# A build-time list scheduler for block-sparse attention followed by a multiplicative FFN

## The chip, the cores and the metric

The kernel runs on one core of one Trainium2 chip. The metric is the device time of one execution in microseconds (us). "Span" is the time from the first to the last instruction in the profiled execution; the timed run is about 2 us longer than its span. One of the first runs of the kernel before took 429.86 us and is left out as an outlier. All ratios below are between runs whose state was fast.

## The reference

Attention with a block mask over 4 batches, 8 heads, 768 positions and head size 64, then an FFN without a nonlinearity other than a product. Cut to what matters:

```python
scores = (q @ k.T) / sqrt(64)             # per batch and head, 768 x 768
mask: |block_i - block_j| <= 1, first or last block row or column, three random blocks a row (32 x 32 blocks)
attn = softmax(where(mask, scores, -1e9))
x = (attn @ v) as [3072, 512]             # heads side by side
out = ((x @ w1) * (x @ w2)) @ w3 @ w_out  # w1, w2: 512 x 1024; w3: 1024 x 1024; w_out: 1024 x 512
```

## The kernel before

All matmuls are bf16. The kernel computes scores transposed (keys on partitions), takes exp on ScalarE (ACT), multiplies by a 0/1 mask on VectorE (DVE), and multiplies by v. `w3 @ w_out` is folded into one matrix on the way (the "weight fold"). The work of TensorE (PE) comes in three kinds, which use the 128 x 128 array in three shapes: scores (64 rows), values (32 columns, four matmuls side by side), and full-array matmuls, that is, the weight fold and the FFN. (The start has two small kinds more, the transposes of q and k and the mask tiles.)

An *attention unit* here is one (batch, 256 queries, half of the heads): three *groups*, each with two score units (4 matmuls each) and one *value third* (24 matmuls), all three thirds accumulating in the same two PSUM tiles `o` and `d`, of which there is one buffer each. A *filler piece* is four FFN matmuls of 512 columns. There are 24 units and 144 FFN pieces. PSUM also has two buffers for scores and two for filler.

```python
def scores(b, t, Q, kp, i):
    s = ps_s.tile([128, 2, 512], F32, ...)            # ps_s: 2 buffers
    for k2 in range(2):
        for h in range(2):
            nc.tensor.matmul(s[:, h, ...], lhsT=qk[64*h:64*h+64, 1, ...], rhs=qk[64*h:64*h+64, 0, ...], ...)
    e = epool.tile([128, 2, 512], BF16, ...)
    nc.scalar.activation(e, s, AF.Exp, scale=1.0 / 8.0)
    nc.vector.tensor_tensor(e, e, mask[:, t, kp:kp + 1, :]..., op=ALU.mult)

def normalize(b, t, Q):                               # frees the accumulators o and d
    nc.scalar.activation(ln, d, AF.Ln)
    nc.scalar.activation(rec[:, 0, :], ln, AF.Exp, scale=-1.0)
    nc.vector.tensor_tensor(X[i][...], o..., rec..., op=ALU.mult)
# [...]
for s, g in enumerate(groups):                        # 72 groups
    scores(b, t, Q, kp, 0)
    scores(b, t, Q, kp, 1)
    if prev is not None:
        values(*prev)                                 # one value third, of the group before
        finish(prev)                                  # after the last third: normalize, queue FFN pieces
    # [... loads of the next batch, transposes of pairs 2 and 3 ...]
    pop(0 if s < 3 else 2)                            # two filler pieces
    prev = g
while fill: pop(1)                                    # the FFN that is left: the tail
```

Before that loop stands the start: q and k come by DMA with a cast to bf16 on GpSimd's (POOL's) queue, DVE builds the 24 x 24 block table in some 25 small instructions, PE expands it to nine mask tiles, which ACT copies, and only then do scores begin. Each engine runs its instructions in the order of the program.

The softmax here doesn't subtract the row's maximum and nothing guards it: scores larger than these inputs give would overflow.

Of the kernel before, what the change touches and what calls it, by code (L numbers as in the profile page):

```python
# [13 lines left out]
PSUM = bass.MemoryType.PSUM  # L14


@with_exitstack
def kernel(
# [15 lines left out]

    nc = tc.nc
# [8 lines left out]
    NT = S // QT  # L44

    def pool(name, bufs, **kw):
# [7 lines left out]
    epool = pool("epool", 6)  # L54
# [3 lines left out]
    apool = pool("apool", 3)  # L58
# [3 lines left out]
    ps_f = pool("ps_f", 2, space=PSUM)  # L62

    order = tc.manual_schedule(
        engines={mybir.EngineType.PE, mybir.EngineType.Activation, mybir.EngineType.DVE}
    )
    order.__enter__()

    nc.scalar.preload_act_table_set("natural_log_exp_and_others")
# [5 lines left out]
    NP = H // 2  # L75
    qn, kn, vn = {}, {}, {}

    rand_sb = const.tile([NB, 6], I32, tag="rand_sb")
    nc.sync.dma_start(out=rand_sb, in_=sampled_blocks.bitcast(I32))

    def load_pair(b, pr, which="qkv"):
        for src, dst, pl, tag in ((qv, qn, nat, "qn"), (kv, kn, nat, "kn"), (vv, vn, natv, "vn")):
            if tag[0] in which:
                t = pl.tile([128, 2, C, D], BF16, tag=tag, name=tag)
                nc.gpsimd.dma_start(out=t, in_=src[b][:, 2 * pr:2 * pr + 2])  # L85
                dst[b, pr] = t
# [8 lines left out]
    def load_w12(ap, t):  # L95
        src = ap.rearrange("(Q g s d) f -> g d Q s f", Q=2, g=4, s=2)
        for g in range(4):
            for Q in range(2):
                nc.gpsimd.dma_start(out=t[32 * g:32 * g + 32, 2 * Q:2 * Q + 2, :], in_=src[g][:, Q])  # L99


    load_pair(0, 0, "qk")
    idf = const.tile([128, 128], F32, tag="idf")
    nc.gpsimd.iota(idf, pattern=[[-1, 128]], base=0, channel_multiplier=1,
                   allow_small_or_imprecise_dtypes=True)
    load_pair(0, 1, "qk")
    hotf = const.tile([NB, C, 128], F32, tag="hotf")
    nc.gpsimd.iota(hotf, pattern=[[1, C], [C, 128]], base=0, channel_multiplier=-BLK,
                   allow_small_or_imprecise_dtypes=True)
    JJ = const.tile([NB, NB], F32, tag="JJ")  # L110
    nc.gpsimd.iota(JJ, pattern=[[1, NB]], base=0, channel_multiplier=0,
                   allow_small_or_imprecise_dtypes=True)
    II = const.tile([NB, NB], F32, tag="II")
    nc.gpsimd.iota(II, pattern=[[0, NB]], base=0, channel_multiplier=1,
                   allow_small_or_imprecise_dtypes=True)
    load_pair(0, 0, "v")
    load_pair(0, 1, "v")
    wo_v = moe_w_out.rearrange("(c r) f -> r c f", r=128)
    nc.gpsimd.dma_start(out=wo_sb, in_=wo_v)

    def load_w3(lo, hi):
        for i in range(lo, hi):
            nc.gpsimd.dma_start(out=w3_sb[:, i, :], in_=moe_w3[128 * i:128 * i + 128, :])

    load_w3(0, 2)
    load_pair(0, 2)
    load_w3(2, 4)
    load_pair(0, 3)
    load_w3(4, NF)
    load_w12(moe_w1, w1_sb)  # L130
    load_w12(moe_w2, w2_sb)

    ident = const.tile([128, 128], BF16, tag="ident")
    nc.vector.tensor_scalar(ident, in0=idf, scalar1=0.0, scalar2=None, op0=ALU.is_equal)
    ones = const.tile([128, 32], BF16, tag="ones")
    nc.vector.memset(ones, 1.0)
    hot = const.tile([NB, C, 128], BF16, tag="hot")
    hot_hi = const.tile([NB, C, 128], BF16, tag="hot_hi")
    nc.vector.tensor_scalar(hot, in0=hotf, scalar1=0.0, scalar2=None, op0=ALU.is_ge)
    nc.vector.tensor_scalar(hot_hi, in0=hotf, scalar1=float(BLK), scalar2=None, op0=ALU.is_lt)  # L140
    nc.vector.tensor_tensor(hot, hot, hot_hi, op=ALU.mult)
    DD = const.tile([NB, NB], F32, tag="DD")
    nc.vector.tensor_sub(DD, II, JJ)

    A = const.tile([NB, NB], F32, tag="A")
    nc.vector.tensor_tensor(DD, DD, DD, op=ALU.mult)
    nc.vector.tensor_scalar(A, in0=DD, scalar1=1.0, scalar2=None, op0=ALU.is_le)
    for src in (II, JJ):
        for val, op in ((0.0, ALU.is_le), (float(NB - 1), ALU.is_ge)):
            t1 = small.tile([NB, NB], F32, tag="m24", name="m24")  # L150
            nc.vector.tensor_scalar(t1, in0=src, scalar1=val, scalar2=None, op0=op)
            nc.vector.tensor_max(A, A, t1)
    rand_f = const.tile([NB, 3], F32, tag="rand_f")
    for r in range(3):
        nc.vector.tensor_copy(rand_f[:, r:r + 1], rand_sb[:, 2 * r:2 * r + 1])
        t1 = small.tile([NB, NB], F32, tag="m24", name="m24")
        nc.vector.tensor_tensor(t1, JJ, rand_f[:, r:r + 1].to_broadcast((NB, NB)),
                                op=ALU.is_equal)
        nc.vector.tensor_max(A, A, t1)
    Ab = const.tile([NB, NB], BF16, tag="Ab")  # L160
    nc.vector.tensor_copy(Ab, A)
# [3 lines left out]
    gp = ps_s.tile([128, 2, 512], F32, tag="s", name="gp")  # L165
    for i, (lo, n) in enumerate(((0, 512), (512, 256))):
        nc.tensor.matmul(gp[:NB, i, :n], lhsT=Ab, rhs=hot2[:, lo:lo + n], start=True, stop=True)
        nc.vector.tensor_copy(G[:, lo:lo + n], gp[:NB, i, :n])
    mask = const.tile([128, NT, 3, 512], BF16, tag="mask")

    def build_mask(t):
        for kp in range(3):
            mp = ps_f.tile([128, 512], F32, tag="f", name="mp")
            for k2 in range(2):
                nc.tensor.matmul(mp[:, k2 * QT:(k2 + 1) * QT], lhsT=hot[:, 2 * kp + k2, :],  # L175
                                 rhs=G[:, t * QT:(t + 1) * QT], start=True, stop=True)
            nc.scalar.copy(mask[:, t, kp, :], mp)  # L177


    QK = {}  # L180

    def transposes(b, pr):
        tp = ps_s.tile([128, 2, 1024], BF16, tag="s", name="tp")
        for x, src in ((0, qn[b, pr]), (1, kn[b, pr])):
            for c in range(C):
                for h in range(2):
                    nc.tensor.transpose(tp[64 * h:64 * h + 64, x, c * 128:(c + 1) * 128],
                                        src[:, h, c, :], ident)
        t = qkt.tile([128, 2, S], BF16, tag="qkt", name="qkt")
        nc.vector.tensor_copy(t, tp[:, :, :S])  # L190
        QK[b, pr] = t

    qd, kd = (x.rearrange("b h (p c) d -> b p c h d", c=C) for x in (q, k))

    def load_pair_t(b, pr):
        load_pair(b, pr, "v")
        t = qkt.tile([128, 2, S], BF16, tag="qkt", name="qkt")
        for x, src in enumerate((qd, kd)):
            n = nat.tile([128, C, 2, D], BF16, tag="nt", name="nt")
            for h in range(2):  # L200
                nc.gpsimd.dma_start(out=n[:, :, h, :], in_=src[b][:, :, 2 * pr + h, :])  # L201
            nc.sync.dma_start_transpose(out=t[:, x, :].rearrange("r (c p) -> r c p", c=C),
                                        in_=n.rearrange("p c h d -> p (c h d)"))
        QK[b, pr] = t

    E = {}

    def scores(b, t, Q, kp, i):
        qk = QK[b, 2 * Q + i]
        s = ps_s.tile([128, 2, 512], F32, tag="s", name="s")  # L210
        for k2 in range(2):
            kc = 2 * kp + k2
            for h in range(2):
                nc.tensor.matmul(s[:, h, k2 * QT:(k2 + 1) * QT],  # L214
                                 lhsT=qk[64 * h:64 * h + 64, 1, kc * 128:(kc + 1) * 128],
                                 rhs=qk[64 * h:64 * h + 64, 0, t * QT:(t + 1) * QT],
                                 start=True, stop=True)
        e = epool.tile([128, 2, 512], BF16, tag="e", name="e")
        nc.scalar.activation(e, s, AF.Exp, scale=1.0 / 8.0)  # L219
        nc.vector.tensor_tensor(e, e, mask[:, t, kp:kp + 1, :].to_broadcast((128, 2, 512)),  # L220
                                op=ALU.mult)
        E[b, t, Q, kp, i] = e
# [3 lines left out]
    def values(b, t, Q, kp):  # L226
        if kp == 0:
            acc["o"] = ps_o.tile([128, 512], F32, tag="o", name="o")
            acc["d"] = ps_o.tile([128, QT], F32, tag="d", name="d")
        o, d = acc["o"], acc["d"]  # L230
        es = [E.pop((b, t, Q, kp, i)) for i in range(2)]
        for k2 in range(2):
            kc = 2 * kp + k2
            first, last = kc == 0, kc == C - 1
# [14 lines left out]
    X = {}  # L249
# [93 lines left out]
    for t in range(NT):  # L343
        build_mask(t)
# [47 lines left out]
    while fill:  # L392
        pop(1)
# [31 lines left out]
```

## Time and profile before

288.69 us, median of three runs (288.67, 288.69, and the outlier). The profiled run took 288.58 us.

| | PE | ACT | DVE |
|---|---|---|---|
| busy, us of the span of 286.8 | 260.8 | 188.8 | 183.8 |
| share | 91% | 66% | 64% |

The first part of the page: busy time by engine; then the span in 40 slices, the busy share of each in tenths, and the clock granted to PE.

```profile
PE 260.8 (91%) x3124; PEld 132.3 (46%) x3124; DVE 183.8 (64%) x296; ACT 188.8 (66%) x250; POOL 71.5 (25%) x105
...
PE   0478888898999999999999999999999999999994
...
PEclk9986999999999999999999999999999999999998
```

PE is the busiest, and nearly full from about 75 us (slice 11) on. Before that it is not. The same by stage; the columns are the stretch, its length, the busy time of PE, PE's weight loads, DVE, ACT and POOL with the number of instructions, the granted clock, the DMA share and GB/s.

```profile
0.00:20.00 20.00, 7.40 (x70) 4.50 (x72) 7.95 (x30) 5.52 (x10) 11.71 (x23) 0.98 0.97 140
20.00:75.00 55.00, 47.71 (x730) 27.05 (x729) 38.57 (x65) 39.08 (x48) 34.34 (x50) 0.95 1.42 166
75.00:240.00 165.00, 163.07 (x2066) 81.98 (x2066) 117.19 (x173) 130.50 (x172) 25.42 (x32) 1.00 0.60 73
240.00:300.00 60.00, 42.57 (x262) 18.79 (x259) 20.05 (x30) 13.74 (x23) 0.00 (x0) 0.97 0.10 36
```

PE's longest waits: who waited for whom, total us, times, longest. PE's first matmul waits 10.6 us for the block table `Ab`.

```profile
PE gp L167 <- DVE Ab L161: 10.6, 1, 10.6
PE s L214 <- ACT e L219: 3.5, 10, 1.1
PE o L244 <- DVE x L260: 1.7, 2, 1.1
```

A busy PE is not a PE at its best. One group on PE's timeline (start, length, engine, line, tiles, count):

```profile
154.42 0.61 PE L214 MATMUL s<-qkt 64*128 64x256 bf16 x8
155.15 0.40 PE L244 MATMUL o<-e,vn 128*32 128x256 bf16 x8
155.37 0.29 PE L241 MATMUL d<-e,ones 128*32 128x256 bf16 x4
155.48 0.41 PE L244 MATMUL o<-e,vn 128*32 128x256 bf16 x8
155.70 0.30 PE L241 MATMUL d<-e,ones 128*32 128x256 bf16 x4
155.93 1.04 PE L303 MATMUL pa<-x,w_sb 128*128 128x512 bf16 x4
156.80 1.03 PE L314 MATMUL pb<-x,w_sb 128*128 128x512 bf16 x4
```

Lengths overlap, since matmuls are pipelined, so starts are what to read. Eight score matmuls could stream in 0.43 us, but the values start 0.73 us after them: 0.1 us for the change to another kind of matmul, and 0.2 us for the accumulators, which the unit before has only just freed. This kernel does scores, values, FFN, scores and so on: nine changes of kind in a unit.

### The profile page before, as it was taken

Reading aid. Unit: us, or ns where it says so; the run is one execution under the profiler, and the core shown is the slowest. Engines: PE = TensorE matmul, PEld = TensorE weight load, DVE = VectorE, ACT = ScalarE, POOL = GpSimd, SP = SyncE. Lnnn points to the kernel's source line nnn. Section 1 sums busy time; section 2 is a strip of 40 time slices with the busy share of each in tenths; the row PEclk is TensorE's granted clock in tenths of the full one; section 3 lists DMA queues with packets and bytes.
Section 4 is the critical chain, followed back from the end, with each engine's and each line's share of the span. In section 5 each row is a group of like instructions: output and inputs, shape, how many; then the busy total and the mean of one; then the engine's idle time right before and its main releaser. Section 6 shows DMA issues by size and latency. Waiting matters only on the chain.

```text
span 286.8 us, 7359 instructions
## 1 busy us (share of the span) xinstructions
PE 260.8 (91%) x3124; PEld 132.3 (46%) x3124; DVE 183.8 (64%) x296; ACT 188.8 (66%) x250; POOL 71.5 (25%) x105
## 2 busy tenths in 40 slices
PE   0478888898999999999999999999999999999994
PEld 0334555454544454445444554445444544444441
DVE  2616786786767776777677767766776677633332
ACT  1088764776788886888877888768887688611310
POOL 8614489374644820066000000000000000000000
PEclk9986999999999999999999999999999999999998
DMA  7999999999999992399912000121000220003003
GB/s 92 151 190 206 208 174 167 178 119 140 135 167 112 144 109 91 79 118 150 160 73 75 2 2 0 39 75 38 3 2 0 77 75 2 0 37 112 0 29 117
DMA packets 70356, 26.16 MB, mean 91 GB/s; under 512 B 58036, under 2 KB 65204, under 8 KB 70324
## 3 DMA queue, kind: packets, MB, share of 16 engines
q0 software_dynamic: 47632, 14.69, 50.9%
q1 hardware_dynamic: 22692, 11.02, 18.5%
q8 instruction: 24, 0.39, 0.6%
q14 instruction: 8, 0.07, 0.1%
HBM read 29.36 MB, written 6.29 MB: 124 GB/s over the span
## 4 chain that ended last, share of the span: by engine, by line
PE 62%; DMA 12%; ACT 12%; DVE 5%; POOL 5%; issue 3%; POOLq 0%; ACTq 0%
PE pa L303 13%; PE o L244 12%; PE pb L314 12%; DMA w_sb<-in_moe_w_dram 11%; PE po L324 10%; ACT e L219 7%; PE s L214 7%; DVE x L260 4%; PE d L241 4%; PE wp L285 3%; ACT rec L259 3%; ACT ln L257 2%; DMA nt<-in_q_dram 2%; POOL w_sb L99 1%; POOL vn L85 1%
## 5 line engine op out<-in xcount | busy, mean ns | idle before, releaser
L219 ACT ACTIVATE e<-s 128x1024 bf16<-128x1024 f32 x144 | 139.1, 1021 | 47.7 <-PE s L214 47.6
L220 DVE TENSOR_TENSOR e<-e,mask 128x1024 bf16<-128x1024 bf16 x144 | 99.0, 691 | 53.8 <-ACT e L219 53.8
L244 PE MATMUL o<-e,vn 128*32 128x256 bf16 x1152 | 54.7, 277 | 5.4 <-DVE x L260 1.7
L214 PE MATMUL s<-qkt 64*128 64x256 bf16 x576 | 46.8, 277 | 3.5 <-ACT e L219 3.5
L303 PE MATMUL pa<-x,w_sb 128*128 128x512 bf16 x192 | 49.7, 381 | 0.0
L314 PE MATMUL pb<-x,w_sb 128*128 128x512 bf16 x192 | 49.2, 379 | 0.0
L316 DVE TENSOR_TENSOR h<-pb,a 128x512 bf16<-128x512 f32 x48 | 33.1, 690 | 20.9 <-PE pb L314 20.9
L324 PE MATMUL po<-wf_sb,h 128*128 128x512 bf16 x192 | 44.5, 380 | 0.0
L306 ACT CAST a<-pa 128x512 bf16<-128x512 f32 x48 | 28.0, 582 | 22.6 <-PE pa L303 22.2
L241 PE MATMUL d<-e,ones 128*32 128x256 bf16 x576 | 42.5, 275 | 0.0
L214 PEld LDWEIGHTS <-qkt 64*128 64x128 bf16 x576 | 22.8, 95 | 34.7 <-issue 32.0
L244 PEld LDWEIGHTS <-vn 128*32 128x32 bf16 x1152 | 27.5, 96 | 22.0 <-issue 19.2
L314 PEld LDWEIGHTS <-w_sb 128*128 128x128 bf16 x192 | 18.7, 98 | 24.1 <-issue 2.6
L201 POOL DMA_DIRECT2D nt<-in_q_dram x24 | 19.7, 824 | 40.2 <-DMA qkt<-nt 35.9
L324 PEld LDWEIGHTS <-h 128*128 128x128 bf16 x192 | 17.5, 98 | 22.3 <-issue 3.4
L303 PEld LDWEIGHTS <-w_sb 128*128 128x128 bf16 x192 | 15.7, 98 | 21.7 <-issue 8.0
L329 DVE COPY ob<-po 128x512 f32<-128x512 f32 x24 | 16.5, 688 | 10.1 <-PE po L324 10.1
L201 POOL DMA_DIRECT2D nt<-in_k_dram x24 | 19.6, 821 | 4.3 <-DMA qkt<-nt 2.3
L260 DVE TENSOR_TENSOR x<-o,rec 128x512 bf16<-128x512 f32 x24 | 16.6, 692 | 1.6 <-ACT rec L259 0.9
L241 PEld LDWEIGHTS <-ones 128*32 128x32 bf16 x576 | 17.3, 98 | 0.3
L285 PE MATMUL wp<-wo_sb,w3t_sb 128*128 128x512 bf16 x64 | 15.2, 380 | 0.0
L177 ACT CAST mask<-mp 128x512 bf16<-128x512 f32 x9 | 4.8, 587 | 13.7 <-PE mp L175 13.7
(56 smaller groups left out, 106.9 us busy)
## 6 DMA issues: line engine op xcount, KB each, us to landing
out_dram<-ob SPq DMA_DIRECT2D x24, 256.0 KB, 2.0
vn<-in_v_dram POOLq DMA_DIRECT2D x16, 192.0 KB, 5.8
nt<-in_q_dram POOLq DMA_DIRECT2D x24, 96.0 KB, 5.6
nt<-in_k_dram POOLq DMA_DIRECT2D x24, 96.0 KB, 5.6
w_sb<-in_moe_w_dram POOLq DMA_DIRECT2D x8, 256.0 KB, 11.2
w_sb<-in_moe_w_dram POOLq DMA_DIRECT2D x16, 128.0 KB, 5.8
wo_sb<-in_moe_w_out_dram POOLq DMA_DIRECT2D x1, 1024.0 KB, 12.0
qn<-in_q_dram POOLq DMA_DIRECT2D x4, 192.0 KB, 7.2
```

Source lines behind the costliest of these rows:

```text
L201: nc.gpsimd.dma_start(out=n[:, :, h, :], in_=src[b][:, :, 2 * pr + h, :])
L214: nc.tensor.matmul(s[:, h, k2 * QT:(k2 + 1) * QT], lhsT=qk[64 * h:64 * h + 64, 1, kc * 128:(kc + 1) * 128], rhs=qk[64 * h:64 * h + 64, 0, ...
L219: nc.scalar.activation(e, s, AF.Exp, scale=1.0 / 8.0)
L220: nc.vector.tensor_tensor(e, e, mask[:, t, kp:kp + 1, :].to_broadcast((128, 2, 512)), op=ALU.mult)
L241: nc.tensor.matmul(d[rows, :], lhsT=ones, rhs=rhs, start=first, stop=last, skip_group_check=True)
L244: nc.tensor.matmul(o[rows, part * QT:(part + 1) * QT], lhsT=vn[b, 2 * Q + i][:, h, kc, 32 * part:32 * part + 32], rhs=rhs, start=first and ...
L260: nc.vector.tensor_tensor(X[i][:, 2 * Q:2 * Q + 2, half * QT:(half + 1) * QT], o.rearrange("p (s n) -> p s n", s=2), rec.to_broadcast((128 ...
L303: nc.tensor.matmul(p, lhsT=w1_sb[:, c, f * 128:(f + 1) * 128], rhs=x[:, c, :], start=c == 0, stop=c == 3)
L306: nc.scalar.copy(a, p)
L314: nc.tensor.matmul(p, lhsT=w2_sb[:, c, f * 128:(f + 1) * 128], rhs=x[:, c, :], start=c == 0, stop=c == 3)
L316: nc.vector.tensor_tensor(hT[:, f, :], p, box["a"], op=ALU.mult)
L324: nc.tensor.matmul(box["o"], lhsT=hT[:, f, n * 128:(n + 1) * 128], rhs=wf_sb[:, f, :], start=f == 0, stop=f == NF - 1)
```

## The change

Its intent: instead of a fixed rotation, a planner in Python runs at build time. Each piece of work is an `Op` with an engine (or a choice of ACT or DVE), an estimated duration, the ops it depends on and the buffer slots it takes. The planner keeps a clock for every engine, always takes the op that can start first, and emits the instructions of all engines in that order. PE's order comes from a rule over three queues (scores, values, filler). Besides, the start is rebuilt: q and k of two head pairs arrive in fp32 on SyncE's (SP's) queue and are cast by ACT or DVE, the block table is built on POOL, seven dummy matmuls run first, mask tiles become filler, and the q and k of batch 1 are transposed on PE instead of by DMA. The exp pool grows from 6 to 13 buffers, and the pool for the first FFN product from 3 to 4. The heart of the diff, cut (most comments are mine):

```diff
-    for s, g in enumerate(groups):
-        scores(b, t, Q, kp, 0)
-        scores(b, t, Q, kp, 1)
-        if prev is not None:
-            values(*prev)
-            finish(prev)
-        [...]
-        pop(0 if s < 3 else 2)
-        prev = g
+class Planner:
+    PATIENCE = 0.2
+    SHARE = 0.6
+    [...]
+    def run_op(self, op, eng, start):
+        if eng == "PE":
+            if op.mode != self.mode:
+                start += 0.1
+            [...]
+            if op.mode == "qk":
+                self.due += self.SHARE
+            elif op.mode == "f":
+                self.due -= op.dur
+    def pick_pe(self):
+        [... rq, rv, rf: when the heads of the score, value and filler queue can start ...]
+        near = max(soon, t + self.PATIENCE)
+        if rq is not None and rq <= near and self.run % 2 == 1:        # scores in pairs
+            return rq, self.qk
+        if rv is not None and rv <= near:
+            op = self.pv[0]
+            whole = all(o.ready() is not None and o.ready() <= rv + 0.3
+                        for o in list(self.pv)[1:3 - op.kp])
+            if op.kp or (whole and self.mode == "qk") or rf is None or rf > near:
+                return rv, self.pv
+        if rf is not None and rf <= near and self.due > 0.3:           # the FFN quota
+            return rf, self.fill
+        if rq is not None and rq <= near:
+            both = self.qk[0].takes[0][0].next_free(1)
+            if (both is not None and both <= rq + 0.45) or rf is None or rf > near:
+                return rq, self.qk
+        if rf is not None and rf <= near:
+            return rf, self.fill
+    [...]
+    def either(dur, emit, deps):
+        return plan.add(Op(("DVE", "ACT"), dur, emit, deps))
+    [...]
+    warm(7)
+    plan = Planner({"PE": 4.3, "ACT": 2.6, "DVE": 4.3, "POOL": 3.4, "SP": 3.0})
-    epool = pool("epool", 6)
+    epool = pool("epool", 13)
-    load_pair(0, 0, "qk")                      # DMA with a cast, POOL's queue
+    nc.sync.dma_start(out=t, in_=src[0][:, 2 * pr:2 * pr + 2])   # fp32; cast later by either()
```

## The prediction

> **What bounds it now.** TensorE: the busy table gives PE 91% (260.8 of 286.8 us), ACT 66%, DVE 64%. The per-stage windows show three parts.
> - 0 to 20 us: first scores only at 19.9 us. q and k come by casting DMA on POOL's queue, the block table is some 25 small DVE instructions (PE's first matmul waits for it until 10.6), all mask evictions go to ACT, the granted clock is 0.80.
> - 20 to 80 us: PE 88% busy; the casting DMA is saturated until 46 us (w1, w2 landed), and the chain of waits runs through these loads.
> - From 80 us PE is always fed; from about 250 a pure FFN tail; 4 us of last copy and store.
>
> Full PE hides waste. In the timeline an attention unit (three groups of scores, values, two FFN pieces) repeats every 9.63 us. At the streaming spacing of the trace its work is three score steps 3 x 0.43, three value thirds 3 x 0.645, six FFN pieces 5.18: 8.4. The other 1.2 us is nine changes of matmul kind (scores to values takes 0.54, values to FFN 0.77: about 0.11 too much each) and one accumulator wait of 0.2. The Trainium skill, "TensorEngine Tiling (Array Packing)", Key Properties, says a change of tiling mode drains the array; the trace agrees, at about 0.11 us.
>
> **What the change does.**
> 1. Startup: q and k of two pairs come in fp32 on SP, cast by DVE/ACT; table on POOL; masks become filler; dummy matmuls warm the clock. First scores at about 9 us: saves 9 to 11 us.
> 2. Whole value thirds and a quota of 1.2 us FFN per score pair: about 7 changes per unit, no accumulator wait: 0.77 instead of 1.2 us, over 24 units 10 us.
> 3. Movable evictions and 13 exp buffers keep PE fed, but the quota hastens attention: a unit of 7.7 us holds 6.6 us of ACT (six exp at 0.97, ln, rec); with DVE and movable evictions both are about 92% full. Fixed orders will disagree with the chip: I allow 0.25 us a unit, 6 us.
> 4. Added: batch 1 transposes on PE (4 x 0.65 us).
> 5. The pure FFN tail grows from 33 to about 50 us; there a pa/pb pair takes 1.87 instead of 1.73 us (two PSUM buffers): about 2 us more.
>
> **Sum (PE), from these durations:** units 24 x 3.23 = 77.5; FFN 576 x 0.216 = 124.4; fold 17; transposes 5; masks 2: 226. Changes of kind 18.5; buffer waits in pure FFN 4; first useful work at 6.5; cold clock 1.5; early starvation (w1, w2 still need 45 to 50 us at the early rate) 4; disagreement with the plan 6; end 4. That is 270 us of span; the timed run is 2 us above the span, but I lean to the low side of the bubbles: **269 us, 8 in 10 between 260 and 280**. Faster by over 2%: 0.90; within 2%: 0.08; slower: 0.02.
>
> **Right if:** first scores before 10 us; attention ends near 205 us; units of 7.8 to 8.2 us holding one block of 72 value matmuls; PE about 93% busy; ACT and DVE over 75% in attention.
>
> **Wrong if:** PE waits on ACT or DVE in attention exceed 10 us (head-of-line blocking); weights land later than planned and block the in-order PE queue at 30 to 55 us; or changes of kind cost less when whole thirds run, which would bring it to 260.

(The clock of 0.80 that it gives for the first 20 us is the view's for 10 to 25 us; the view for 0 to 20 says 0.98.)

## The result

276.22 us, median of four runs (276.08 to 276.32), against 289.14 us for the kernel before, the median of its four runs with the outlier (288.67 to 289.60 without it). The ratio is 0.9558, 95% interval 0.9536 to 0.958: 4.4% faster.

The page of the kernel after, the same lines:

```profile
PE 265.9 (97%) x3228; PEld 135.1 (49%) x3228; DVE 186.5 (68%) x299; ACT 180.0 (66%) x241; POOL 63.0 (23%) x100
...
PE   6999999899999999999999999999999999999994
...
PEclk9999999999999999999999999999999999999999
```

By stage, and PE's longest waits:

```profile
0.00:20.00 20.00, 17.18 (x144) 7.91 (x148) 12.31 (x25) 12.31 (x15) 11.76 (x28) 1.00 1.01 200
20.00:75.00 55.00, 52.87 (x796) 29.09 (x787) 38.13 (x63) 39.05 (x54) 31.98 (x49) 1.00 1.28 175
75.00:240.00 165.00, 165.00 (x2137) 84.66 (x2135) 117.48 (x185) 126.90 (x170) 19.24 (x25) 1.00 0.41 58
240.00:300.00 60.00, 30.82 (x160) 13.40 (x158) 18.57 (x28) 1.76 (x4) 0.00 (x0) 0.97 0.09 35
```

```profile
PE warm L278 <- DVE warm_sb L239: 1.2, 1, 1.2
PE s L466 <- ACT e L473: 1.1, 4, 0.4
```

PE is busy 17.2 instead of 7.4 us in the first 20, and without a break from 75 us on; the view of its waits from 75 us on is empty. Part of PE's timeline in the steady part:

```profile
126.80 0.61 PE L466 MATMUL s<-qkt 64*128 64x256 bf16 x8
127.34 1.04 PE L597 MATMUL pa<-x,w_sb 128*128 128x512 bf16 x4
128.22 1.03 PE L614 MATMUL pb<-x,w_sb 128*128 128x512 bf16 x4
129.17 0.40 PE L508 MATMUL o<-e,vn 128*32 128x256 bf16 x8
129.40 0.28 PE L505 MATMUL d<-e,ones 128*32 128x256 bf16 x4
129.51 0.39 PE L508 MATMUL o<-e,vn 128*32 128x256 bf16 x8
129.73 0.28 PE L505 MATMUL d<-e,ones 128*32 128x256 bf16 x4
129.95 0.61 PE L466 MATMUL s<-qkt 64*128 64x256 bf16 x8
```

Here the value third at 129.17 stands alone. The rule prefers whole units, but of the 28 value blocks from 75 us on 13 are single thirds and 11 are whole.

**A ledger of PE's time.** Since PE is full in both kernels, busy shares cannot show where the time went. I took the start times of all matmuls in the trace and counted three things. *Streaming*: each matmul at its warm spacing inside a run of its own kind (0.2158 us for 512 columns of the full array; 0.107 us for 256 columns, shared by the two score matmuls or four value matmuls that run side by side; 0.056 us for a transpose of 128 columns, shared by two for q and k). *Changes of kind*: the number of blocks of one kind, times 0.097 us. *The rest* ("other loss") is waits, short stalls and cold clock, that is, stretches in which matmuls are about twice their warm spacing apart. A block is counted whole in the stage in which it starts. The traces of e1 to e8 lack 32 to 48 records of full-array matmuls, seen as pieces of three instead of four; they are counted as streamed. The 0.097 is measured: from 75 us on, in both kernels, each direction of change costs the same to two nanoseconds wherever nothing else is waited for. Score to value matmul is 199 ns from start to start, where 107 are the score matmul's own streaming; value to FFN or to score 205 (107); FFN to score 312 (216); FFN to value 309 (216); score to FFN 202 (107): 92 to 98 ns each.

| us of PE | before | after |
|---|---|---|
| before the first matmul | 10.6 | 1.2 |
| streaming of real work | 223.4 | 226.3 |
| streaming time of the dummies (7 x 0.216) | 0 | 1.5 |
| changes of kind: 218 and 221 blocks | 21.1 | 21.4 |
| other loss until 20 us | 7.8 | 9.7 |
| other loss 20 to 75 us | 11.9 | 5.3 |
| other loss from 75 us | 7.7 | 5.3 |
| after the last matmul | 4.3 | 3.8 |
| sum = span | 286.8 | 274.5 |

Of the 12.3 us gained, the two early "other loss" rows and the first three rows together make 9.7, although streaming grew by 2.9 us, nearly all of it batch 1's transposes on PE. Other loss from 75 us on gives 2.4, the end 0.5. The number of changes of kind did not fall at all: the steady part has fewer (140 blocks after 75 us instead of 162), the first 75 us more (81 instead of 56), since masks, fold and transposes are dealt out in single pieces.

### The profile page after: what moved, and what is told of

Same layout as the page of the kernel before. It is cut to its first block, busy times and chain, and to the rows that moved or that the text cites. A ratio compares the mean times of both kernels' runs of the same rounds, so it can differ in the third digit from the quotient of the medians.

```text
span 274.5 us, 7499 instructions
## 1 busy us (share of the span) xinstructions
PE 265.9 (97%) x3228; PEld 135.1 (49%) x3228; DVE 186.5 (68%) x299; ACT 180.0 (66%) x241; POOL 63.0 (23%) x100
## 4 chain that ended last, share of the span: by engine, by line
PE 91%; ACT 3%; DVE 3%; POOL 1%; issue 1%; POOLq 0%; ACTq 0%
PE pa L597 16%; PE pb L614 16%; PE po L635 16%; PE s L466 15%; PE o L508 13%; PE d L505 6%; PE wp L578 4%; ACT e L473 3%; PE tp L375 3%; PE mp L446 1%; DVE e L477 1%; PE w3p L561 1%; POOL A L257 0%; DVE wf_sb L284 0%; DVE qkt L284 0%
## 5 line engine op out<-in xcount | busy, mean ns | idle before, releaser
L473 ACT ACTIVATE e<-s 128x1024 bf16<-128x1024 f32 x144 | 141.4, 1028 | 31.4 <-PE s L466 31.3
L508 PE MATMUL o<-e,vn 128*32 128x256 bf16 x1152 | 52.4, 278 | 0.8 <-DVE x L541 0.5
L466 PE MATMUL s<-qkt 64*128 64x256 bf16 x576 | 48.9, 279 | 1.4 <-ACT e L473 1.1
L466 PEld LDWEIGHTS <-qkt 64*128 64x128 bf16 x576 | 22.1, 95 | 31.4 <-issue 26.8
L635 PEld LDWEIGHTS <-h 128*128 128x128 bf16 x192 | 17.3, 98 | 22.3 <-issue 3.6
L317 POOL DMA_DIRECT2D vn<-in_v_dram x16 | 11.5, 722 | 48.4 <-PE d L505 46.8
L284 DVE CAST a<-pa 128x512 bf16<-128x512 f32 x27 | 18.6, 688 | 5.6 <-PE pa L597 5.6
L532 ACT ACTIVATE ln<-d 128x256 f32<-128x256 f32 x24 | 9.2, 385 | 17.4 <-PE d L505 17.2
L505 PEld LDWEIGHTS <-ones 128*32 128x32 bf16 x576 | 16.4, 98 | 0.5
L578 PE MATMUL wp<-wo_sb,w3t_sb 128*128 128x512 bf16 x64 | 16.5, 381 | 0.0
L284 ACT CAST a<-pa 128x512 bf16<-128x512 f32 x21 | 12.2, 582 | 5.7 <-PE pa L597 5.7
```

Of the source, the lines that this page charges most:

```text
L284: (nc.scalar.copy if eng == "ACT" else nc.vector.tensor_copy)(dst, src)
L466: nc.tensor.matmul(s[:, h, k2 * QT:(k2 + 1) * QT], lhsT=qk[64 * h:64 * h + 64, 1, kc * 128:(kc + 1) * 128], rhs=qk[64 * h:64 * h + 64, 0, ...
L473: nc.scalar.activation(e, box["s"], AF.Exp, scale=1.0 / 8.0)
L505: nc.tensor.matmul(d[rows, :], lhsT=ones, rhs=rhs, start=first, stop=last, skip_group_check=True)
L508: nc.tensor.matmul(o[rows, part * QT:(part + 1) * QT], lhsT=vn[b, 2 * Q + i][:, h, kc, 32 * part:32 * part + 32], rhs=rhs, start=first and ...
L578: nc.tensor.matmul(box["p"], lhsT=w3t_sb[:, j, i * 128:(i + 1) * 128], rhs=wo_sb[:, j, :], start=j == 0, stop=j == NF - 1)
```

## The experiments

Theory A: PE is fed, so a schedule costs what its changes of kind cost, 0.097 us each, plus the start. Theory B: what pays is that the planner picks by readiness, so that PE never waits; a fixed rotation would bring waits back, whatever its number of changes. Theory C: the FFN quota (`SHARE`, how much FFN time is due per score unit) pays. A rival for the start: an early start is given back, because the weights still land at 45 to 50 us. "Blocks" below are counted over the whole kernel, weight transposes and FFN as one kind. All twelve kernels gave correct results.

### Fixed rotations in the planner: e1, e2, e3, e12

The edit to the kernel after (shown in short, comments mine): from the 42nd score unit on, PE's pick is replaced by a fixed string, q a score unit, v a value third, f a filler piece. Everything else, the planner's order for ACT and DVE included, is planned anew around it.

```diff
     def pick_pe(self):
         t = self.free["PE"]
+        want = self.fixed()      # None before the 42nd score unit and after the last
+        if want is not None:     # else the queue that CYCLE names next
+            r = want[0].ready()
+            return None if r is None else (max(r, t), want)
+    CYCLE = "qqvff"              # e1;  e2 "qqfvf";  e3 "qqfffqqvvvqqfff";  e12 "qqffqqvvvqqff", aligned to units
```

**e1**, before's rotation:

> The kernel after, but from the 42nd score unit on PE follows a fixed rotation like before's: score pair, one value third, two FFN pieces (nine changes of matmul kind per attention unit); 242 blocks of one kind in all instead of 221 (weight transposes counted with the FFN). Theory A (a change of kind costs about 0.097 us of PE whatever the schedule, and PE is fed): 21 more blocks, +2.0 us, about 278.2 us. Theory B (the gain of the steady part is the planner's free choice by readiness; a rotation blocks): PE waits on ACT or DVE come back and it is over 281. Theory C (the FFN quota is what pays): the rotation has six FFN pieces per unit again, as before, so it loses the whole steady gain of 4.6 us, about 281.

Measured 292.98 us (290.86 to 295.21), ratio 1.0133 (1.0065 to 1.0201). Theory A misses by 15 us. The ledger from 75 us on: 161 blocks, 15.6 us of changes, but 22.3 us of other loss instead of 5.3. PE's waits show the accumulators:

```profile
PE o L529 <- DVE x L562: 9.0, 9, 1.3
```

The next unit's first third follows the last third of the unit before after one score pair and two pieces. In the kernel before, whose `ln`, `rec` and `x` stand right behind the values in program order, that distance nearly suffices: 17 of its 53 score-to-value changes from 75 us on waited, 3.2 us in all. In e1 the planner puts other ready work ahead of them: once `rec` is done at 161.4 us, DVE still finishes a mask multiplication and does an `h` before it starts `x` at 162.49. From 75 us on these waits are 8.5 of the 17.0 us more; the rest is spread over smaller waits and is not taken apart here.

**e2**, the two pieces parted:

> The same rotation with the two FFN pieces parted: score pair, FFN piece, value third, FFN piece (twelve changes per unit), 292 blocks instead of 221. Theory A: 71 more blocks, +6.9 us, about 283. Theories B and C: no different from the nine-change rotation, which has the same work and the same FFN share per unit.

Measured 283.77 us (283.75 to 284.50), ratio 0.9822 (0.9794 to 0.985). From 75 us on: 211 blocks, 20.5 us of changes, other loss 6.3. This is what theory A says for a schedule without added waits: +6.9 us expected over the kernel after, +7.5 measured. e1 and e2 do the same work at the same FFN share and differ by 9 us, so theory C cannot explain the difference.

**e3**, value thirds whole:

> The same rotation with whole values: score pair, three FFN pieces, score pair, three value thirds, score pair, three FFN pieces (six changes per unit), 191 blocks instead of 221. Theory A: 30 fewer blocks, -2.9 us, about 273.3, faster than the kernel after. Theory B: slower than after, by PE waits. Theory C: slower than after, about 281, since the FFN share is six pieces per unit.

Measured 348.53 us (346.50 to 348.92), ratio 1.204 (1.1997 to 1.2083). The run was built wrongly for its purpose, and is instructive for it: the three thirds in a block were the last one of one unit and the first two of the next. PE's waits, and one such block on its timeline:

```profile
PE o L529 <- DVE x L562: 45.3, 18, 3.4
```

```profile
152.12 0.41 PE L529 MATMUL o<-e,vn 128*32 128x256 bf16 x8
...
152.46 0.39 PE L529 MATMUL o<-e,vn 128*32 128x256 bf16 x8
152.68 0.28 PE L526 MATMUL d<-e,ones 128*32 128x256 bf16 x4
155.45 0.62 PE L529 MATMUL o<-e,vn 128*32 128x256 bf16 x8 [2.49 <-DVE x L562]
```

PE stands in its queue behind a value matmul that needs the accumulators, until ACT has done `ln` and `rec` and DVE `x`. And after the gap the same 12 matmuls take 0.60 us (155.45 to the next pair at 156.05 in the trace) instead of 0.34 (152.12 to 152.46): the clock has dropped, so the wait is paid for again in slow matmuls. By my count of the starts, matmuls at about twice their warm spacing add some 14 us from 75 us on. The whole run was granted 0.926.

**e12**, the mended rotation, thirds of one unit always together:

> A fixed rotation as in the two of the first call, mended: value thirds of a unit always whole and never across the accumulator's turn: score pair, two pieces, score pair, three value thirds, score pair, two pieces, from the 42nd score unit on. 193 blocks instead of 221. If only changes of kind and accumulator waits matter: 28 fewer blocks, -2.7 us, about 273.5. If attention with four pieces a unit is too tight for ACT and DVE (a unit is 7.3 us of PE and holds 6.6 us of ACT before any eviction), PE waits in every unit and it is 280 or more.

Measured 282.6 us (281.93 to 283.05), ratio 0.9771 (0.9739 to 0.9802). It has the fewest blocks of these (193, and 112 from 75 us on), and yet it is 6.4 us slower than the kernel after: from 75 us on changes cost 10.9 us (13.6), but other loss is 14.5 (5.3). From 100 to 220 us ACT is busy 104.5 of 120 us, in the kernel after 95.1, and PE's score blocks lose 257 ns each instead of 136, the value blocks 156 instead of 143. PE's waits name the cause of about half of what the score blocks lose beyond the changes: from 75 us on, scores wait ten times, 4.4 us in all, for an exp to free a score buffer (in the kernel after: never). So the time that the expectation's last sentence gives holds, but PE does not wait in every unit. Theory A falls as stated: counting changes is right only for schedules that add no wait, and here a rotation, even a good one, adds them.

### Striking one condition: e5 and e6

```diff
-            if op.kp or (whole and self.mode == "qk") or rf is None or rf > near:
+            if op.kp or (whole and self.mode == "qk"):
```

e6 has besides:

```diff
-    PATIENCE = 0.2
+    PATIENCE = 0.15
```

> The kernel after with one condition struck from its PE rule: a first value third starts only when the whole unit's probabilities are ready and PE has just done scores, and no longer also when the filler is not ready. 195 blocks of one kind instead of 221, value thirds whole from 75 us on. Theory A (PE is fed, so what is left in the steady part is the changes of kind at about 0.097 us): 26 fewer blocks, -2.5 us, about 273.7. Rival (the mixed order is what keeps PE from waiting; fewer changes come with longer waits for the accumulator or the filler's PSUM buffers, as in the two rotations with 252 and 201 blocks that ran 17 and 72 us over the kernel after): 277 or more.

(The 252 and 201 blocks are slips: e1 and e3 have 242 and 191.)

Measured 274.67 us (273.75 to 274.87), ratio 0.9494 (0.9466 to 0.9521).

> The same with the planner's patience 0.15 us instead of 0.2, that is, PE may pass over a head of a queue that is ready 0.15 us later than another. 206 blocks. Theory A: 15 fewer than the kernel after, -1.5 us, about 274.8. Rival: 277 or more. The planner's own table puts it 4 us below the strict version; if the chip follows it, the table knows waits that my count of blocks does not.

Measured 272.79 us (272.19 to 273.02), ratio 0.9432 (0.9407 to 0.9457). This beats both kernels: its interval lies below that of the kernel after. But fewer changes are only a part of it: from 75 us on, changes and other loss are 13.6 and 5.3 us in the kernel after, 11.0 and 7.2 in e5, 11.9 and 4.8 in e6. e5 has the fewest blocks (195, e6 206) and gives most of that back in waits, so the count does not decide between the two; the planner's table did put them in this order. e6's steady part comes close to the schedule that I had predicted for the change itself: all its 19 value blocks from 75 us on are whole. A stretch of its timeline, with a block of three whole thirds from 124.99 to 127.08:

```profile
122.08 0.61 PE L466 MATMUL s<-qkt 64*128 64x256 bf16 x8
122.62 1.04 PE L597 MATMUL pa<-x,w_sb 128*128 128x512 bf16 x4
123.49 1.03 PE L614 MATMUL pb<-x,w_sb 128*128 128x512 bf16 x4
124.45 0.61 PE L466 MATMUL s<-qkt 64*128 64x256 bf16 x8
124.99 0.40 PE L508 MATMUL o<-e,vn 128*32 128x256 bf16 x8
...
126.86 0.28 PE L505 MATMUL d<-e,ones 128*32 128x256 bf16 x4
127.08 0.61 PE L466 MATMUL s<-qkt 64*128 64x256 bf16 x8
```

The first two rows are means over 14 units, from the first value matmul of the 9th unit to that of the 23rd:

| | before | after | e6 |
|---|---|---|---|
| us per attention unit | 9.62 | 9.10 | 8.24 |
| FFN pieces per unit | 6.0 | 5.7 | 4.9 |
| last attention matmul starts, us | 248.1 | 241.3 | 223.7 |
| FFN pieces after it | 38 | 33 | 49 |

### The quota: e7

```diff
-    SHARE = 0.6
+    SHARE = 0.8
```

> The kernel after with the FFN quota 0.8 instead of 0.6 us per score unit, 215 blocks. If the quota only moves FFN work between the attention part and the tail, PE being fed in both, it is 275.6 by the block count, within 1 us of the kernel after. If the quota is what keeps a reserve of FFN for the whole of attention, PE runs out of filler, waits for ACT, and it is 280 to 285.

Measured 288.51 us (286.15 to 289.09), ratio 0.9963 (0.9916 to 1.0011): all of the gain is gone, more than I expected. Changes cost about what they cost in the kernel after (215 blocks), but other loss in the whole run is 34 us instead of 20. The timeline shows why (PE, and the one DVE instruction that makes the next FFN input):

```profile
101.28 0.61 PE L466 MATMUL s<-qkt 64*128 64x256 bf16 x8
...
102.79 0.39 PE L466 MATMUL s<-qkt 64*128 64x256 bf16 x4 [0.90 <-ACT e L473]
...
103.38 0.68 DVE L541 TENSOR_TENSOR x<-o,rec 128x512 bf16<-128x512 f32 x1
...
104.01 0.51 PE L466 MATMUL s<-qkt 64*128 64x256 bf16 x4 [0.82 <-ACT e L473]
```

PE has no filler left: it does four score units in a row, the last two waiting for an exp to free a score buffer (0.90 and 0.82 us), until `x` is done at 104.06 and FFN work exists again (the next FFN matmul starts at 104.85). With a larger quota the reserve of filler is used up early and PE then runs at ACT's pace. So the quota matters when it is too large: it spends the reserve too fast. This part of theory C holds. Only one such place is shown here; how much of the 34 us comes from it was not added up.

### The start: e4, e8, e11

**e4**: the kernel before with the new start alone, written by hand into its loop.

```diff
-    load_pair(0, 0, "qk")  [...]  load_pair(0, 1, "qk")  [... table on DVE ...]
+    [... fp32 loads on SP, table on POOL, warm(7), four casts on ACT and DVE, as in the kernel after ...]
-    for t in range(NT):
-        build_mask(t)
+    build_mask(0)              # masks 1 and 2 inside the loop, after groups 1 and 3; evicted by ACT and DVE in turn
```

> The kernel before with only the new start: q and k of the first two pairs in fp32 on SP and cast by ACT and DVE, block table on POOL, dummy matmuls, first three masks before the loop and the others inside it, evicted by ACT and DVE in turn. Nothing else changed. Theory A (startup is the largest part of the gain): first scores at 10 to 11 us instead of 19.9, and the run 8 to 10 us shorter, about 280. Rival: the weights still land at about 46 us and PE takes them in order, so the early start is given back as waits before 75 us and the run gains 4 us or less, about 285.

Measured 291.41 us (288.92 to 292.06), ratio 1.0062 (1.0013 to 1.0112): no gain. First scores came at 14.0 instead of 19.9 us, but by the fifth group nothing of it was left:

| start of scores of group, us | 0 | 4 | 8 | 12 | 18 |
|---|---|---|---|---|---|
| before | 19.9 | 29.3 | 41.8 | 55.8 | 73.7 |
| e4 | 14.0 | 29.0 | 42.4 | 56.3 | 74.3 |
| after | 9.1 | 22.4 | 37.5 | 48.7 | 69.3 |

In e4 the first scores wait for exps (0.90 and 0.52 us), the mask tiles, put into the loop at fixed places, hold PE for their evictions (0.67, 0.67 and 0.45 us), and PE's matmuls ran mostly at the cold spacing until 33 us (before: until 25.8). This shows that the head start is not kept by itself. It does not show that no hand order could keep it.

**e8**: the start delayed in the kernel after, by dummy matmuls.

```diff
-    warm(7)
-    plan = Planner({"PE": 4.3, [...]
+    warm(55)
+    plan = Planner({"PE": 14.7, [...]
```

> The kernel after with 55 dummy matmuls instead of 7, so PE's real work starts at about 14.6 us instead of 4.8; the plan is told so. Theory A (an early start is kept, since PE is fed to the end): of the 9.9 us the start's own waits absorb 3 to 5, and the run is 5 to 7 us longer, 281 to 283. Rival (weights arriving at 45 to 50 us set the pace of the first part, so an earlier start is given back, as in the kernel before with the new start): 2 us longer or less, at most 278.

Measured 282.83 us (282.15 to 283.88), ratio 0.9785 (0.9747 to 0.9824). First scores at 17.2 instead of 9.15 us, 8.05 later, and the run is 6.6 us longer. Under the planner most of an early start is kept to the end, and the rival falls: the arrival of the weights does not set the pace there.

**e11**: without the seven dummies.

```diff
-    warm(7)
```

> The kernel after without the seven dummy matmuls. If they buy a warm clock for the first real work (masks, transposes, first scores), the first 20 us lose about 1 to 2 us and the run is 1 to 2 us longer; since the trace of the kernel after still shows cold spacing at 9 to 19 us (first scores 0.61 us for four matmuls), I expect less: 276 to 277.

Measured 275.88 us (275.70 to 276.24), ratio 0.9547 (0.9523 to 0.9572): no different. The trace of the kernel after says why: all seven dummies are 0.43 us apart, twice the warm 0.216, and the transposes and scores that follow run at the cold spacing until about 20 us with them or without. (In the traces of e1, e3 and e10, which have the same seven dummies, the masks and first transposes ran warm from 5.6 us on, and PE was cold again by 9.8 us at the latest. So in some executions seven are enough, but not for long.) In e8 the spacing drops to 0.216 us after ten dummies, at 5.4 us.

### The cost of a change by itself: e9

The kernel before, no planner, one piece before and one after the values:

```diff
         scores(b, t, Q, kp, 1)
+        pop(0 if s < 3 else 1)
         if prev is not None:
             values(*prev)
         [...]
-        pop(0 if s < 3 else 2)
+        pop(0 if s < 3 else 1)
```

> The kernel before with its two filler pieces of a group parted: scores, one piece, values, one piece, instead of scores, values, two pieces. 287 blocks of one kind instead of 218, the same work, no planner. Theory A (0.097 us a change): +6.7 us, about 296; if the 0.2 us accumulator wait of each unit goes away, as values come later, 3 us less, about 292. If the changes of kind cost nothing that other waits do not hide, no change.

Measured 291.92 us (291.40 to 292.64), ratio 1.0103 (1.0072 to 1.0133): +2.7 us. From 75 us on the ledger reads 217 blocks instead of 162, which is +5.3 us, and other loss 5.1 us instead of 7.7: the accumulator waits (3.2 us before) are gone, since the values now come a piece later. Both terms of the expectation are there, and they nearly cancel; the total alone would have been read as "a change costs 0.04 us".

### Evictions tied to engines: e10

```diff
-    def either(dur, emit, deps):
-        return plan.add(Op(("DVE", "ACT"), dur, emit, deps))
+    def either(dur, emit, deps, eng="DVE"):
+        return plan.add(Op(eng, dur, emit, deps))          # "ACT" for the masks and the first FFN product
```

> The kernel after with the movable evictions tied down as in the kernel before: mask and the first FFN product on ACT, all other copies on DVE; the planner orders anew. 231 blocks instead of 221. Theory A: +1.0 us by the blocks, about 277. Rival (spreading evictions over ACT and DVE is a main source of the gain): +5 us or more, 281 or over.

Measured: two fast runs, 278.88 and 282.34 us, two slow ones above; ratio of the fast runs 0.9709 (0.9631 to 0.9788). So it is slower than the kernel after, by 2.7 and 6.1 us in the two runs; one lies between the two theories, the other fits the rival. In the trace of the 278.88 us run the loss from 75 us on is 22.6 instead of 18.9 us, only 0.6 of it changes. Movable evictions are worth some us; how many, this run leaves open.

## Why the prediction was right, and where a step of it was not

The time (269, range 260 to 280) and the direction held; the measured 276.2 is 7 us above the 269. That it came so close is partly luck, since terms of the sum that were wrong by 3 to 6 us cancel in part (below). PE was busy 97%, not 93%, and from 75 to 240 us ACT 77% and DVE 71%, where over 75% was predicted for both. Point by point:

- **"First scores at about 9 us: saves 9 to 11 us."** Right: 9.15 against 19.88 us, and e8 shows that a start 8 us later costs 6.6 us. But the saving was kept only with the planner's order behind it; in e4's order by hand it was lost.
- **"Whole value thirds and a quota of 1.2 us FFN per score pair: about 7 changes per unit, no accumulator wait [...] over 24 units 10 us."** This step failed in size. In the kernel after there are 7.9 changes per unit from 75 us on (140 blocks over 17.7 units of scores; before 9.2), thirds are often split, and in the whole kernel the changes rose from 218 to 221. From 75 us on, changes and waits together fell by 4.5 us: 2.1 from 22 fewer changes and 2.4 from other loss, of which the accumulator waits (3.2 us before) are the largest item.
- **"The quota hastens attention: a unit of 7.7 us"; "attention ends near 205"; the tail "grows [...] to about 50 us".** Wrong. A unit took 9.10 us with 5.7 FFN pieces (before: 9.62 and 6.0), attention ended at 241 us, and the tail shrank to 33 pieces. I read the quota as what sets the FFN share. It only puts FFN first when some is due; the rule takes filler also whenever two score buffers are not soon free. e7 shows that the quota does bind when raised, and e6 comes near what I had described, at 8.2 us and 4.9 pieces a unit.
- **"Disagreement with the plan 6."** Too large: no wait of PE is listed from 75 us on. With the buffer waits that I put at 4, 10 us were set aside where 5.3 were lost. **Startup terms** (6.5 + 1.5 + 4 = 12) were too small: 1.2 + 1.5 + 9.7 + 5.3 = 17.7. These two, 2.9 us more for the changes (21.4, not 18.5), 0.3 more of streaming and 0.2 less at the end turn my sum of 270.5 into the measured 274.5 of span. The last 3 us are that I went from 270 of span to 269 of time, "leaning to the low side", where the timed run is 2 us longer than the span; nothing had been measured for that lean.
- **"The trace agrees, at about 0.11 us"** for a change of tiling (the Trainium skill, "TensorEngine Tiling (Array Packing)", Key Properties): a cost of this size is there at every change, 92 to 98 ns; that it is a drain, no run here isolates.
- **"Dummy matmuls warm the clock."** Of no use at this number. The Trainium skill, "TensorE: Matmul & The Clock Gate", Part 1, puts the rise at about 4 us of sustained activity; e8 agrees (4.2 us after the first dummy). Seven dummies last only 3.0 us, three of the traces have a short warm stretch after them, and e11 shows that the time gains nothing.

Open: why the rule of the kernel after keeps taking 5.7 pieces per unit while the slightly changed one takes 4.9; the other half of what e12's score blocks lose; and the size of the gain from movable evictions. Two rivals were not tested: no run has the planner with the 6 exp buffers of the kernel before, or the old loop with 13, so the buffers' share of the gain is not known; and none has the planner with the old start, so what the planner gives alone in the first 75 us is not known either.

## What to carry to other kernels

When PE is full in the trace, split its time into streaming, changes of kind and the rest, from start times and not from busy shares; here 21 us of 287 were changes of tiling shape that no wait list shows. Fewer changes pay only where they add no wait: waits for a single accumulator (e3) or for score buffers (e12) cost more than the changes saved, so let buffers and readiness decide the order and count the changes second. An early start is worth something only if the in-order queues behind it are arranged so that nothing gives it back.

## What the Trainium skill lacked or had wrong

- "TensorEngine Tiling (Array Packing)", Key Properties, says that a change of tiling mode drains the array, but gives no cost: it is 92 to 98 ns here, for all six directions between the three kinds. Between full-array transposes and full-array matmuls there is none (56 ns after a transpose, 216 ns after a matmul, their own streaming).
- "TensorE: Matmul & The Clock Gate", the closing table, warns of PE-idle gaps above about 3 us between bursts of matmuls. In e8 PE fell back to the cold spacing at 22.4 us and stayed there until 29 us, with no gap between matmuls longer than 0.47 us since 15 us, and in e3 the matmuls after a gap of 2.49 us were cold. The page's section on a second failure mode does tell of short idles that have this effect, but not how short or how many. In e8 the matmuls' warm streaming time filled 48 to 57% of PE from 16 to 22 us, before the fall, counted in steps of 2 us; whether that share is what decides, no run here isolates.
- The same page, Part 1, warns that the recorded clock events are unreliable. The profile of the kernel after shows a granted clock of 1.00 for the first 20 us, while the spacing of the dummies (427 ns instead of 216) says half.
